# Fifty one-column matmuls ahead of TensorE's first transposition, and a new fixed order of all engines

## The chip, the cores and the metric

The kernel runs on one core of one Trainium2 chip. A core has five engines that run side by side: TensorE (PE, with its weight loads shown apart as PEld), VectorE (DVE), ScalarE (ACT), GpSimd (POOL) and SyncE (SP). SP, and in places POOL and ACT, issue DMA transfers. The metric is the device time of one execution in microseconds (us), lower is better. Times are medians of several executions; the profile is of one more execution.

## The reference, cut to what matters

Two stages follow each other. The first is a retention layer without softmax over 8 batches, 8 heads, 576 positions and 64 values a head; its output, 4608 tokens of 512 values, goes through a two-layer network whose gate is h times cos(h).

```python
scores = scale * np.matmul(q, k.transpose(0, 1, 3, 2))          # scale = 1/8
ret = scores * Dmat                 # gamma_h ** (i - j) where i >= j, else 0
x = np.matmul(ret, v).transpose(0, 2, 1, 3).reshape(4608, 512)
h = x @ w_in                        # 512 x 2048
out = (h * np.cos(h)) @ w_out       # 2048 x 512
```

## The kernel before, in words

**Tiling.** The tokens are cut into nine blocks of 512. Block j takes its rows from two batches: a "unit" is one batch and one third of its positions, (batch, part), and two units of one part make a block. For a unit, `load` (L585) brings q, k and v to staging tiles stgq, stgk, stgv (issued by SP). POOL, and for the first units DVE and ACT, scale and cast them to natk, qnat, natv (L624 and L575, at the very start L574 on ACT). natk and qnat are transposed to kt and qt, by TensorE for the first two blocks (`tpe`, L648, against the identity idn) and by DMA for later ones (`txb`). One phase of TensorE, `scores`, multiplies qt and kt; DVE multiplies by the decay mask into pt (L743); the state sums (natv times natk) run in the same phases; another phase, `outputs`, makes the unit's x (pt times natv, qt times the state copies sba, sbb, sbr), which ACT and DVE copy to xt. All these small matmuls are recorded at L694. They have 64 rows and 64 columns of weights and 64 or 128 columns of data, and go through four parts of the array at once. Here such a phase is called an **attention phase**.

**The network.** The first layer reads win (four slabs, loaded by POOL at L888) and xt; blocks 0 to 2 compute it directly (`mlp1`, L908), blocks 3 to 8 with a seven-product scheme (`seven1`, L1037). The second layer reads gt and wout (loaded by POOL at L892) with the same scheme (`wino2`, L1177). Their matmuls have 128 rows, 128 columns of weights and mostly 256 columns of data. Every matmul is two instructions on TensorE's instruction stream, the weight load and the multiplication.

**What sets the order.** The program is recorded as tasks of a graph (class `Graph`). A string, `ORDER`, gives every task a rank, two characters each (`lay`). `run` then goes through the tasks with a model of the engines and DMA queues: at each step the engine whose next task by rank can start earliest gets it. Only the resulting order of each engine, the choice of buffers and some added waits go into the program; on the chip, semaphores decide when things start. `run` also holds a model of TensorE's instruction supply: `seen` counts instructions, a block k of 256 is asked for when instruction 128 + 256k starts, and the instructions from 450 + 256k on can start when that block is `usable`. `FETCH` and `SHARES` are numbers of that model.

**Filling.** While TensorE waits early in the program, `emit` calls `warm(n)` (L515), which puts in n matmuls of the constant tile `one` with 512 columns (L517); `fill` (L193) picks n from the length of the gap that the model sees. They write the spare bank `wb`, and their results are not used. The first gap is the one ahead of the first transposition.

Of the kernel before, what the change touches and what calls it, by code (L numbers as in the profile page):

```python
# [99 lines left out]
def ap(t, size, p0, n, off, *dims):  # L100
    return bass.AP(t, p0 * size + off, [[size, n]] + [list(d) for d in dims])
# [29 lines left out]
class Graph:  # L131


    BACKLOG, FIRST = 4000, 6000
    SHARES = (0.65, 0.30)
    FETCH = (3200, 1500, 2550, 2000)
    SINCE = 3000

    def __init__(self, pools):
# [113 lines left out]
    def run(self):  # L253
        self.reset()
        free = {e: 0.0 for e in ("pe", "act", "dve", "pool", "sp")}
        todo = {e: sorted((t for t in self.tasks if t.eng == e), key=lambda t: -t.prio) for e in free}
        seen, usable, whole = 4, {}, [False] * 8
        dma_free, port_free = 2500.0, {"dve": 0.0, "pool": 0.0}
        est, order, last, mode, held = {t: 0.0 for t in self.tasks}, [], None, "", None
        slow = sum(t.eng == "pool" and t.dma is not None for t in self.tasks)  # L260
# [111 lines left out]
class Kernel:  # L372
# [10 lines left out]
    SLABS = ((0, 'q', 0, 100), (2, 'q', 1, 101), (1, 'k', 1, 102), (3, 'k', 1, 103))  # L383
    NEXT = 2
    ORDER = (
        "#####$#$#$#%#%#$#######%#&#&#%#$#&#'#)#(#'#)#,#+#'#.#7#/#*#/#'#+#*#,#(#-#.#&#&#%#*#)#(#-#(#)#*#0#2#0#1#3"
        "#2#1#,#7#V#8#/#7#'#(#,#)#-#.#G#@#K#H#*#0#/#L#C#J#G#+#2#1#+#N#O#K#L#M#N#P#E#S#P#T#H#Q#,#3#5#f#[#^#R#-#8#6"
        "#b#W#V#L#.#<#;#5#+#4#U#I#S#3#-#5#E#>#E#6#.#6#@#8#>#4#5#<#=#4#?#<#3#;#>#6#=#H#A#J#;#2#:#:#1#9#B#9#@#9#0#8"
        "#C#=#C#R#G#R#F#?#F#Q#F#P#I#B#I#D#<#D#A#:#A#?#;#B#M#D#O#4#7#9#:#/#>#=#0#?#@#1#A#G#6#m#o#j#k#m#l#l#_#r#u#s"
        "#a#`#_#d#y#p#^#i$'#w#]#Q#[#v#b#s$'#l$%$/#s$/#Z#N#W$3#v$1#e#Z#c$+#r$-#j#^#h$$#i#{#x#d#u$.#q$0#_#S#]$1#t$."  # L390
        "#[#O#X$(#m$&#W#J#T#{#h#|#\\#T#\\$*#n$)#Y#M#Y$&#k$(#|#g#x$,#p$+#X#K#U#y#f#z#a#U#`#z#j$##c#X#f#w#c#t#i#]#g$)"
        "#o$*#Z#b#V#a#q#e#o#n#`#d#Y#q#t#r#k#p#e#g#h#\\$#$%$$#n#u#v#8$-$0#w#O#2#D#B#5#I#C#3#E#H#<$5$7$7$9$8$3$6#z$?"
        "$$$#$@$%#|#4#9#F#K#7#J#N#=#;#M#L#C#:#>#O#R#A#Q#T#?#@#S#P#F$>$B$?$<$A$@$F$,$+$G$'$&$\\$?$Z$O$0$I$[$>$V$_$C"
        "$[$S$6$Q$U$7$P$K$*$D$Z$=$U$J$($G$M$-$J$L$1$L$R$5$N$Q$3$K$Y$<$T$X$:$R$T$@$Y$2$4$,$6$5$;$>$=$4$8#x$2$:$:$;"
        "$<#y$9$=#{$A$D$B$C$E$C#`$H$I$)#P$N$H$F$.$/$P$2$4$V$;$9$W$8$S#B#G#W#Z#E#X#V#D#M#Y#`#Q#J#N#^#a#H#c#[#I#L#\\"
        "#d#V$]$X$W$B$A$b$D$G$c$E$^$o$l$k$M$R${$Y$Z$|$W$s#S#K#f#l#R#e#j#U#X#g#o#[#T#\\#i#t#Y#w#x#W#Z#k#q#g%'$w$x$^"
        "$a%.$l$m%/$f$|#U$E#]$M#_$d#b$n$`$b$e$f$`$F$k$J$f$K$i$n$N$r$p$b#p$p$m$Q#h$y$V$t$s$O$t$P$x$U$r$v$S$z$u$[#n"
        "$w$q$X#m%($_$y%%$\\%&$]%*$e%#%)$`%-${$j#s%+$z$d#r%1$k%(%,$c%3$i%2$h%%%0$g%4%&$n#v%6%'$p#u%9$q%.$]$_$\\$a$c"
        "$o$O$g$d$e$H$^$a$h$h$i$I$g$j$L$l$m$j%#%$$v#o$q$u$T#f%)%+%1%/%=$r%>$s%@$v%5%A$t%D%8%%$(%B%4%,$*%L%$%?%E$y"
        "%G$|%M%#%>%H${%K%<%($&%N%=%.$)%P%&%A%S%*%U%-%Y%1%G%V%2%]%H%7$,%Z%F%<$.%d%=%P%[%3%_%6%`%9%L%^%5%c%K%>$1%e"  # L400
        "%N%E$2%g%?%Q%$%*%0%2%:%6%9%7%5%7$o%:%?%3%<%F$z%;%C$w%O%T%B%I%J%;$&%X%\\%4#q%8%-%,$u$x%Q%)%'%R%+%@#d#]#{#y"
        "#a$$#z#^#e$##|#i#b#k$%$0#h$3$-#_#c$'$+#v%W%D%C%/%0%a%8%:%b%;%J%M%S%V%T%k%B%m%D%o%G%[%n%C%q%Y%H$8%r%Z%K$<"
        "%u%M%b%z%N%{%O&'%S%e&$%P&(%d%W$?&%%c%Z$A&-%Y%i&&%R&)%U&*%T%f&,%V&3%j%`$C&.%h%c$D&6%e%q&/%X&1%]&2%\\%k&4%^"
        "&9%p%h$F&7%n%d$E&>%i%v%E%I%U%X%^%]%W%\\%f%i%A%p%x%`%l%t%L%j%s%I&#&+%g%y%|%a$?&0&5%_$=%h%O%R%@%F%v%Q%[%w%J"
        "%_#l#m$7$/#n$:$5#p#j$4$6#|#s#t$9$=#w$@$B#r#u$;$>$+&8%o%m%b%a&<%f%l&=%g%r%s%u%{%x&@%j&E%o&C%n%|&D%m&I&%%x"
        "$H&H&$%v$G&O%u&,&M%s&P%w&V&#&/&Q%y&W&1&($N&U&.&&$K&a&+&;&X&$&Y&%&[&'&6&]&*&c&5&1$P&\\&4&2$R&h&5&A&b&,&g&0"
        "&i&3&=&f&/&j&?&8$S&k&<&9$U&t&:&D%l%t%w&#&)%y&+&'&;&?%k&A&B%z&G&L%q&:&F%p&R&Z&0&K&N&*$7&^&`&-$:&J&&&(%r%t"
        "&S%z%{&T%|&-$-$6#z$4$I$L$%$,$8$0$J$O$##y#x#{$W$[$9&_&2&3&)&d&e&.&7&8&9&>&:&l&4&n&7&q&<&F&o&6&r&C&K$\\&s&B"
        "&@$Y&y&?&G&u&;&v&=&z&D&Q&x&A'&&K&L$_&{&H&C$X'*&I&R'#&B')&E'(&G&V''&F'/&W&O$`',&P&M$^'6&P&\\'4&N'5&Q'8&T&f"
        "'7&R';&]&X$a':&^&[$b'>&Z&h&@&E&I&L&M&J&S&N&m&p&>&|'$&O'%'-&J&w'+&H'0'2&Y'.'3&X$@'9'=&V$>$1$$$2$'$Q$V$)$5"  # L410
        "$*$($M$T$3$.$<$/$]$Z$;'1&[&T&Z&U'<&S&_&U&`&b&c&e&d'?&W'A&Y'B&\\&i'E&^'K&n&j$e'D&k&g$d'O&c&q'F&]'H&_'P&d&t"
        "'I&`'N&p&e$c'L&r&k$f'U&i&x'M&b'T&h'Q&o'#'W&l'[&w&p$g'Y''&y$i'^&r&{'Z&n'a&t'`&s'$']&q'b&|&u$h'f'+&z$j'e&v"
        "'&&a&l&j&m&g&v&s&o'@'G&a'S'V&u'R'X&m'C'J&f'\\'c'%'_'d'($A'i'j'#$C&y&z')','*'/'-'0'g'h&w&x'o'p'.$E$B'k'n&{"
        "&|'l'm'$'q'r'1'2$F$D's't'3'%'&'v'u'5'4$H$G"
    )
# [59 lines left out]
    def emit(self, order):  # L475
# [217 lines left out]
    def mm(self, out, lhs, rhs, start=True):  # L693
        return lambda e: e.matmul(out(), lhs(), rhs(), start=start, stop=True, skip_group_check=True)  # L694
# [191 lines left out]
    def load_w(self, which, s, gate, prio):  # L886
# [4 lines left out]
        else:  # L891
# [459 lines left out]
```

## Time and profile before

| | |
|---|---|
| median of 3 executions | 282.84 us (282.12 to 283.46) |
| the profiled execution, its own time | 284.13 us |
| its span, first to last instruction | 282.4 us |
| TensorE busy | 270.7 us (96%), 4136 matmuls |
| VectorE, ScalarE, GpSimd busy | 80%, 63%, 57% |
| read from HBM, written | 36.70 MB, 9.44 MB |

The profiled execution took 1.29 us more than the median, and 1.73 us of it lie outside the span. In the timeline each row is a start (us from the span's start), a length, an engine, a line of the kernel, the tiles out<-in, the shape and how many instructions; in brackets stand the idle time of the engine ahead of the row and what ended it. "issue" there means that nothing in the profile held the engine back. A row's length runs to the end of its last matmul, and rows of TensorE overlap by some 0.17 us, since matmuls are pipelined.

### The profile page before, as it was taken

The numbers are of one execution on the slowest core, as the hardware profiler recorded it, in microseconds if no ns is written. First come the engines' busy times: TensorE is split into PE (matmuls) and PEld (weight loads), VectorE is DVE, ScalarE is ACT, GpSimd is POOL, SyncE is SP. The second block draws the span as 40 slices with busy tenths as digits, with TensorE's granted clock in tenths as the row PEclk, the third lists the DMA queues.
The fourth block names the chain that finished last, engine by engine and source line by source line (L and its number), as shares of the span: only waits on it lengthen the run. The fifth ranks groups of instructions, "written<-read, shape, count | busy, mean of one in ns | idle before, by whom it ended". The sixth has DMA issues, their size and how long they took to land.

```text
span 282.4 us, 9745 instructions
## 1 busy us (share of the span) xinstructions
PE 270.7 (96%) x4136; PEld 219.9 (78%) x4136; DVE 227.3 (80%) x394; ACT 177.5 (63%) x367; POOL 161.2 (57%) x180
## 2 busy tenths in 40 slices
PE   6779989999999999979999999999999999999995
PEld 2457568888885468868888888888888888888884
DVE  3666889988974998868997996688759899997764
ACT  4346767255247765669469875885778865778530
POOL 4640872167377683897568757981375667216330
DMA  7999999999999999999999997979816090410016
GB/s 199 249 192 262 273 171 163 300 243 263 179 187 245 204 264 206 181 221 176 251 192 208 279 238 134 168 194 175 194 32 123 6 163 2 159 69 0 2 74 224
DMA packets 122731, 49.91 MB, mean 177 GB/s; under 512 B 84800, under 2 KB 118592, under 8 KB 122688
## 3 DMA queue, kind: packets, MB, share of 16 engines
q1 hardware_dynamic: 118176, 44.84, 74.8%
q0 software_dynamic: 4224, 4.19, 9.6%
q8 instruction: 32, 0.52, 0.8%
q10 hardware_dynamic: 288, 0.26, 0.3%
q14 instruction: 11, 0.09, 0.1%
HBM read 36.70 MB, written 9.44 MB: 163 GB/s over the span
## 4 chain that ended last, share of the span: by engine, by line
PE 84%; DMA 8%; POOL 3%; issue 2%; SPq 1%; DVE 1%; ACT 1%; DVEq 0%; ACTq 0%
PE bk L1177 38%; PE bk L1037 26%; PE bk L908 11%; PE bk L694 8%; DMA stgq<-in_q_dram 3%; DMA win<-in_moe_w_in_dram 3%; DMA stgk<-in_k_dram 3%; POOL natv L624 1%; SPq L585 1%; POOL qnat L624 1%; POOL gt L1026 1%; POOL win L888 0%; ACT xt L574 0%; DVE sq L1020 0%; PE bk L648 0%
## 5 line engine op out<-in xcount | busy, mean ns | idle before, releaser
L1026 POOL TENSOR_TENSOR gt<-sq,cb 128x512 bf16<-128x512 f32 x48 | 55.8, 1172 | 49.1 <-ACT cb L1022 27.0
L908 PE MATMUL bk<-xt,win 128*128 128x256 bf16 (+1 forms) x288 | 46.3, 308 | 1.8 <-DMA win<-in_moe_w_in_dram 0.9
L624 POOL TENSOR_TENSOR natv<-stgv,wv 128x512 bf16<-128x512 f32 x36 | 37.5, 1046 | 12.5 <-DVE s L1108 4.8
L920 DVE TENSOR_TENSOR gt<-bk,cb 128x256 bf16<-128x256 f32 (+1 forms) x72 | 34.5, 507 | 12.0 <-ACT cb L917 9.3
L917 ACT ACTIVATE cb<-bk 128x256 bf16<-128x256 f32 (+1 forms) x72 | 31.2, 455 | 19.6 <-PE bk L908 16.5
L624 POOL TENSOR_TENSOR qnat<-stgq,wq 128x512 bf16<-128x512 f32 x32 | 33.5, 1052 | 16.7 <-DVE s L1114 5.6
L1037 PE MATMUL bk<-xt,win 128*128 128x256 bf16 x288 | 41.0, 273 | 0.0
L1020 DVE TENSOR_TENSOR sq<-bk,sq 128x512 f32<-128x512 f32 x48 | 32.5, 684 | 8.9 <-PE bk L1037 5.0
L908 PEld LDWEIGHTS bk<-xt,win 128*128 128x128 bf16 x288 | 26.8, 98 | 15.3 <-DVE pt L743 1.2
L743 DVE TENSOR_TENSOR pt<-bk,tr 128x512 bf16<-128x512 f32 x48 | 31.1, 682 | 8.4 <-PE bk L694 8.1
L575 POOL CAST natk<-stgk 128x512 bf16<-128x512 f32 x34 | 20.7, 614 | 28.2 <-DMA stgk<-in_k_dram 15.7
L1177 PE MATMUL bk<-wout,gt 128*128 128x256 bf16 x288 | 36.7, 273 | 0.0
L1026 DVE TENSOR_TENSOR gt<-bk,cb 128x512 bf16<-128x512 f32 x48 | 32.3, 682 | 4.0 <-ACT cb L1022 3.8
L1177 PE MATMUL bk<-wout,s 128*128 128x256 bf16 x288 | 35.6, 273 | 0.0
L1177 PE MATMUL bk<-tw,s 128*128 128x256 bf16 x288 | 35.4, 273 | 0.0
L574 ACT ACTIVATE sq<-bk 128x512 f32<-128x512 f32 x48 | 27.7, 595 | 10.0 <-PE bk L1037 8.8
L1022 ACT ACTIVATE cb<-sq 128x512 bf16<-128x512 f32 x48 | 30.0, 632 | 5.4 <-DVE sq L1020 2.9
L1022 ACT ACTIVATE cb<-bk 128x512 bf16<-128x512 f32 x48 | 28.4, 598 | 6.7 <-PE bk L1037 3.7
L1177 PEld LDWEIGHTS bk<-tw,s 128*128 128x128 bf16 x288 | 28.0, 98 | 3.6 <-DVE pt L743 0.3
L1037 PEld LDWEIGHTS bk<-xt,win 128*128 128x128 bf16 x288 | 27.9, 98 | 3.6
L1177 PEld LDWEIGHTS bk<-wout,gt 128*128 128x128 bf16 x288 | 27.6, 98 | 3.7 <-issue 0.2
L1177 PEld LDWEIGHTS bk<-wout,s 128*128 128x128 bf16 x288 | 27.7, 98 | 3.5
(80 smaller groups left out, 436.5 us busy)
## 6 DMA issues: line engine op xcount, KB each, us to landing
stgq<-in_q_dram SPq DMA_DIRECT2D x16, 512.0 KB, 6.1
out_dram<-os SPq DMA_DIRECT2D x16, 512.0 KB, 4.4
stgk<-in_k_dram SPq DMA_DIRECT2D x20, 256.0 KB, 5.6
stgv<-in_v_dram SPq DMA_DIRECT2D x20, 256.0 KB, 5.4
stgk<-in_k_dram SPq DMA_DIRECT2D x6, 512.0 KB, 6.9
stgv<-in_v_dram SPq DMA_DIRECT2D x6, 512.0 KB, 7.4
win<-in_moe_w_in_dram POOLq DMA_DIRECT2D x4, 512.0 KB, 8.0
wout<-in_moe_w_out_dram POOLq DMA_DIRECT2D x4, 512.0 KB, 7.5
```

What stands on the lines that cost most here:

```text
L574: return self.one(eng, dur, lambda e: e.activation(dst(), src(), AF.Copy), r=r, w=w, **kw)
L624: self.one(eng, 610 if eng == "dve" else 1030, lambda e, out=out, inp=inp, tab=tab, col=col, hs=hs: e.tensor_tensor(out(), inp(), ap(tab, ...
L694: return lambda e: e.matmul(out(), lhs(), rhs(), start=start, stop=True, skip_group_check=True)
L743: self.one("dve", 610, lambda e, r=r, b=b, pt=pt: e.tensor_tensor(ap(self.at(pt), 1024, 0, 128, 512 * r, [64 * ny * ny, 8 // ny // ny], [1 ...
L908: inst = e.matmul(ap(self.at(bk), 512, 0, 128, 0, [1, n]), ap(self.WIN, 4 * DFF, 0, 128, c * DFF + 128 * f, [1, 128]), ap(self.at(xt), 204 ...
L917: self.one("act", n - 15, lambda e: e.activation(ap(self.at(cb), TB, 0, 128, 0, [1, n]), ap(self.at(bk), 512, 0, 128, 0, [1, n]), AF.Sin, ...
L920: self.one("dve", 75 + n / 0.96, lambda e: e.tensor_tensor(ap(self.at(gt), NF * TB, 0, 128, f * TB + 256 * h0, [1, n]), ap(self.at(bk), 51 ...
L1020: self.one("dve", 610, lambda e: e.tensor_tensor(half(src), self.at(bank).ap(), half(src), ALU.add), r=[(bank,)], w=four(src))
L1022: self.one("act", 530 if name else 490, lambda e: e.activation(self.at(cb).ap(), ap(self.at(src), size, 0, 128, 0, [1, 512]), AF.Sin, bias ...
L1026: self.one(eng, 1120 if name else 610, lambda e: e.tensor_tensor(ap(self.at(gt), NF * TB, 0, 128, (8 * n + 2 * g) * TB + 256 * h, [TB, 2], ...
L1037: inst = e.matmul(ap(self.at(bank), 512, 0, 128, 256 * f, [1, 256]), l(c, f), rr(c), stop=True, skip_group_check=True, start=(first and f ...
L1177: inst = e.matmul(place(bank, tt), l(f, tt), rr(f), stop=True, skip_group_check=True, start=(first and f == 0 and tt < len(bank)))
```

## The change

The class's numbers change, `emit` calls a new function `pad` ahead of TensorE's first task (and still `warm`), `fill` picks fewer large matmuls for the first gap, the planner's count starts 100 instructions later, and `ORDER` is another string of the same length, so that nearly every engine's order differs.

```diff
-    BACKLOG, FIRST = 4000, 6000
-    SHARES = (0.65, 0.30)
-    FETCH = (3200, 1500, 2550, 2000)
+    BACKLOG, PAD = 4000, 50
+    SHARES = (0.80, 0.35)
+    FETCH = (3200, 1500, 3550, 5550)
...
-        return int(0.6 * (gap - 150) / 220 if seen else (gap - 1400) / 430)
+        return int(0.6 * (gap - 150) / 220 if seen else (gap - 3000) / 430)
...
-        seen, usable, whole = 4, {}, [False] * 8
+        seen, usable, whole = 4 + 2 * self.PAD, {}, [False] * 8
...
-                    usable[k] = max(a + self.FETCH[0], dma_free + self.FETCH[1]) + self.FETCH[2] + self.FETCH[3] * (a < 45000)
+                    usable[k] = max(a + self.FETCH[0], dma_free + self.FETCH[1] * (a > 8000)) + self.FETCH[2 + (8000 < a < 45000)]
...
     ORDER = (
-        "#####$#$#$#%#%#$#######%#&#&#%#$#&#'#)#(#'#)#,#+#'#.#7#/#*#/#'#+#*#,#(#-#.#&#&#%#*#)#(#-#(#)#*#0#2#0#1#3"
+        "###$###$#$###%#$#####%#%#&#&#%#$#%#'#(#'#(#)#*#)#'#,#*#-#+#/#'#+#,#.#)#/#.#&#&#&#+#(#*#-#(#)#*#0#1#1#2#0"
...
             if t.eng == "pe":
                 gap = t.start - warm
+                if not warm:
+                    self.pad(self.G.PAD)
                 if gap > 400 and self.wb.left:
...
+    def pad(self, n):
+        def mm(e):
+            for _ in range(n):
+                inst = e.matmul(ap(self.at(self.wb), 512, 0, 1, 0, [1, 1]), ap(self.ONE, 128, 0, 128, 0, [1, 1]),
+                                ap(self.ONE, 128, 0, 128, 0, [1, 1]), start=True, stop=True, skip_group_check=True)
+            return inst
+        self.P.add("pe", mm, r=["one"], w=[("bk", self.wb.slot)])
```

Lines of the changed kernel are ten higher than before from `emit` on (L648 is L658, L694 is L704, L908 is L918, L1037 is L1047, L1177 is L1187). The numbers of real matmuls stay the same; of the matmuls on `one` there were 24 of 512 columns and are 20, and the 50 of one column come on top, so the program has 46 matmuls, or 92 instructions, more ahead of all that follows.

**Place 1, the start of TensorE.** Before, the thirteen fillings are followed by the transposition of k:

```order
L517 MATMUL bk<-one 128x512 x13
L648 MATMUL bk<-idn,natk 128x128 x4
L648 MATMUL bk<-idn,qnat 128x128 x8
L648 MATMUL bk<-idn,natk 128x128 x4
L517 MATMUL bk<-one 128x512 x2
L694 MATMUL bk<-qt,kt 64x128 x16
```

In the changed kernel, the pads and five fillings stand there, then both halves of q:

```order
L519 MATMUL bk<-one 1x1 x50
L527 MATMUL bk<-one 128x512 x5
L658 MATMUL bk<-idn,qnat 128x128 x8
L527 MATMUL bk<-one 128x512 x2
L658 MATMUL bk<-idn,natk 128x128 x8
L527 MATMUL bk<-one 128x512
L704 MATMUL bk<-qt,kt 64x128 x32
```

Eight fillings gave way to fifty pads, and the transpositions of q moved ahead of those of k. On POOL, which issues the loads of win, the first casts stood like this before:

```order
L575 CAST natk<-stgk 128x512
L624 TENSOR_TENSOR natv<-stgv,wv 128x512
L575 CAST natk<-stgk 128x512
L624 TENSOR_TENSOR natv<-stgv,wv 128x512
L888 DMA win<-in_moe_w_in_dram 128x4x512 x2
```

Now, on POOL at the same place:

```order
L585 CAST natk<-stgk 128x512
L634 TENSOR_TENSOR natv<-stgv,wv 128x512 x2
L585 CAST natk<-stgk 128x512
L898 DMA win<-in_moe_w_in_dram 128x4x512 x2
L634 TENSOR_TENSOR natv<-stgv,wv 128x512 x2
```

The second cast of k changed places with the second scaling of v; the same four operations stand ahead of the first load of win. SP's first twelve loads keep their order.

**Place 2, the first attention work of unit (2, 0).** TensorE before, from the last transpositions for block 1 to that unit's state sums and scores, with work of both layers between:

```order
L648 MATMUL bk<-idn,qnat 128x128 x4
L908 MATMUL bk<-xt,win 128x256 x4
L1177 MATMUL bk<-wout,gt 128x256 x8
L908 MATMUL bk<-xt,win 128x256 x4
L648 MATMUL bk<-idn,natk 128x128 x4
L1177 MATMUL bk<-tw,s 128x256 x16
L908 MATMUL bk<-xt,win 128x256 x8
L1177 MATMUL bk<-tw,s 128x256 x8
L694 MATMUL bk<-natv,natk 64x64 x16
L694 MATMUL bk<-qt,kt 64x128 x16
L1177 MATMUL bk<-wout,s 128x256 x8
```

TensorE in the changed kernel, up to the same state sums and scores:

```order
L918 MATMUL bk<-xt,win 128x256 x12
L658 MATMUL bk<-idn,natk 128x128 x4
L918 MATMUL bk<-xt,win 128x256 x8
L658 MATMUL bk<-idn,qnat 128x128 x4
L918 MATMUL bk<-xt,win 128x256 x8
L658 MATMUL bk<-idn,qnat 128x128 x4
L918 MATMUL bk<-xt,win 128x256 x8
L704 MATMUL bk<-natv,natk 64x64 x16
L918 MATMUL bk<-xt,win 128x256 x4
L704 MATMUL bk<-qt,kt 64x128 x16
L1187 MATMUL bk<-wout,gt 128x256 x8
```

The attention work came 56 matmuls of the real work earlier, ahead of all of the second layer, and is cut in two by four matmuls of the first.

**Place 3, the middle of the program.** TensorE before, from the products of one unit to the scores and state sums of the next:

```order
L694 MATMUL bk<-pt,natv 64x64 x32
L694 MATMUL bk<-qt,sba 64x64 x12
L694 MATMUL bk<-natv,natk 64x64 x16
L694 MATMUL bk<-qt,sba 64x64 x12
L1177 MATMUL bk<-wout,s 128x256 x16
L1037 MATMUL bk<-xt,win 128x256 x4
L1037 MATMUL bk<-xs,tx 128x256 x4
L694 MATMUL bk<-qt,kt 64x64 x32
L694 MATMUL bk<-natv,natk 64x64 x16
L1037 MATMUL bk<-xt,tx 128x256 x4
```

TensorE in the changed kernel, the same work:

```order
L704 MATMUL bk<-pt,natv 64x64 x32
L704 MATMUL bk<-qt,sba 64x64 x12
L704 MATMUL bk<-natv,natk 64x64 x16
L704 MATMUL bk<-qt,sba 64x64 x12
L1187 MATMUL bk<-wout,s 128x256 x16
L1047 MATMUL bk<-xt,win 128x256 x4
L704 MATMUL bk<-qt,kt 64x64 x32
L704 MATMUL bk<-natv,natk 64x64 x16
L1047 MATMUL bk<-xs,tx 128x256 x4
L1047 MATMUL bk<-xt,tx 128x256 x4
```

Here four matmuls of the network moved behind the scores; counted from the program's start, the row of scores begins at matmul 1812 before and 1854 now (the first is number 0).

Over the whole program, TensorE goes from the network to an attention phase and back 30 times from unit (2, 0) on, and 33 times in the changed kernel.

More of the change, by code (lines that the diff above doesn't have):

```diff
@@ L391 @@
[L391 to L410, printed above, removed]
@@ new lines @@
+        "#3#3#,#6#3#7#0#5#'#(#,#)#-#.#G#A#I#G#*#/#0#K#C#M#I#+#2#1#+#O#Q#L#K#N#M#P#E#S#f#T#I#Q#,#5#3#V#K#Z#O#-#9#6"
+        "#]#R#`#V#.#8#:#2#-#6#U#J#S#E#?#D#<#5#@#5#/#4#;#4#:#4#.#8#D#=#C#A#;#?#=#6#<#9#7#;#?#9#=#>#8#>#:#2#9#8#1#7"
+        "#B#<#B#J#F#O#F#@#E#N#G#P#H#B#H#@#:#A#L#D#J#C#>#F#R#H#R#4#7#;#<#0#>#=#3#@#A#/#D#B#8#e#m#`#c#j#h#c#W#r#x#s"
+        "#_#`#X#e#o#n#^#l#u#z#k#]#i#y#e#x#w#c#v#|#k$$#g#[#f$'#m$'#b#Z#g$/#r$-#d#X#_$,#u$0#v#b#t$0#t$2#W#L#T#z#h#{"
+        "#^#S#[$-#s$.#[#P#W$+#q$,#\\#Q#Y$&#l$%#p#^#m#{#g#|#u#a#s$(#o$*#Y#N#U$##i$##X#M#V$$#j$&#a#U#]$)#n$(#_#T#\\$*"
@@ L415 @@
+        "'J&_'N&r&f$d'L&n&j$e'T&m&y'P&e'S&i'Z&r'$'Y&l'`&z&s$g'W&w&v$i'f&w'+'X&k'^&p'_&q'''\\&o'a&{&u$h'b'*&z$j'd&t"
+        "'(&g&j&h&l&t&p&i&s'?'A&`'D'U&v'O'[&n'Q'R&g'c'e'%'V']&x$@'h'i'#$B&|'&','-'#')'/'0'g'j&y&x'k'o'.$C$F'm'n&|"
+        "&{'l'p'$'q'r'2'1$E$D's't'3'%'&'v'u'5'4$H$G"
     )
@@ L895, in load_w @@
         self.one("pool", 1000, fn, r=gate, w=[(which, s)] if which == "win" else [(which, s, 0), (which, s, 1)],
-                 sem=f"{which}{s}", dma=2750 if which == "win" else 3000, tail=900, prio=prio)
+                 sem=f"{which}{s}", dma=3350 if which == "win" else 3450, tail=500, prio=prio)
     def mlp1(self, j, f, ses, prio):
```

28 lines of the change are left out of this document (20 added, 8 removed).

## The prediction

> **What bounds the kernel now.** I read the page first, for which engine is full, then the chain that ended last, then TensorE's timeline for the places where it stands still.
>
> ```profile
> PE 270.7 (96%) x4136; PEld 219.9 (78%) x4136; DVE 227.3 (80%) x394; ACT 177.5 (63%) x367; POOL 161.2 (57%) x180
> DMA  7999999999999999999999997979816090410016
> q8 instruction: 32, 0.52, 0.8%
> ```
>
> The third row (packets, MB, share of 16 engines) is not what I expected to need. 4136 matmuls and 4136 weight loads on 32 packets are 258 instructions a packet, of 16 KB each: TensorE's program comes to it by DMA in pieces, over engines that the DMA row shows full (a digit is a fortieth of the span, 7 us) for some 200 us.
>
> The chain's early part, in order of time (start, length, what):
>
> ```profile
> 10.45 0.61 POOL natk L575
> 11.06 1.00 POOL natv L624
> 12.06 0.89 POOL win L888
> 12.95 8.27 DMA win<-in_moe_w_in_dram
> 21.70 8.43 DMA stgq<-in_q_dram
> 32.23 2.05 POOL natv L624 x2
> ...
> 38.69 0.76 ACT xt L574
> ```
>
> Up to 34.3 us the end is set by transfers: POOL issues the loads of win, the landing of the second at 21.2 lets SP load unit (0, 1), and POOL's scaling of that ends at 34.3. From there to the end the chain lies on TensorE. Now TensorE's timeline, the rows ahead of and behind each pause:
>
> ```profile
> 1.12 4.82 PE L517 MATMUL bk<-one 128*128 128x512 bf16 x13 [1.12 <-DVE lg L543]
> 7.48 0.40 PE L648 MATMUL bk<-idn,natk 128*128 128x128 bf16 x4 [1.54 <-ACT natk L574]
> 17.71 1.47 PE L908 MATMUL bk<-xt,win 128*128 128x256 bf16 x12 [0.88 <-DMA win<-in_moe_w_in_dram]
> 20.40 0.50 PE L908 MATMUL bk<-xt,win 128*128 128x256 bf16 x3 [0.68 <-issue]
> 37.22 0.28 PE L694 MATMUL bk<-natv,natk 64*64 64x64 bf16 x7
> 38.22 0.22 PE L694 MATMUL bk<-natv,natk 64*64 64x64 bf16 x3 [0.71 <-issue]
> 123.73 0.26 PE L694 MATMUL bk<-natv,natk 64*64 64x64 bf16 x9
> 125.45 0.25 PE L694 MATMUL bk<-natv,natk 64*64 64x64 bf16 x7 [1.46 <-issue]
> ```
>
> The last three pauses (0.68, 0.71 and 1.46 us) fall inside a run of equal matmuls and end by "issue": no data was missing. Here is how many matmuls (behind the x) had started by each:
>
> ```profile
> 0.00:20.30 20.30, 14.67 (x221) 1.00 1.01 214
> 20.30:38.10 17.80, 16.82 (x246) 1.00 1.09 243
> 38.10:125.30 87.20, 85.59 (x1386) 1.00 1.13 221
> ```
>
> Two instructions to a matmul make 492 and 2772 between the pauses. With the separate waits that the program holds (100 on TensorE), 512 and 2816 fit, 2 and 11 times 256. I take the pauses for **borders of instruction blocks**: TensorE had used up one block and the next had not come. There are 31 such borders, one in 123 to 126 matmuls, and three of them cost 2.85 us together. When do they cost something? The same view over some stretches of about one block (stretch, length, busy time and count of PE, the granted clock, the share of the DMA engines, GB/s):
>
> ```profile
> 32.62:37.50 4.88, 4.74 (x111) 1.00 0.86 199
> 50.00:55.00 5.00, 5.00 (x127) 1.00 1.18 308
> 119.85:123.99 4.14, 4.14 (x138) 1.00 1.14 263
> 156.75:161.37 4.62, 4.62 (x128) 1.00 1.20 290
> 125.30:265.00 139.70, 139.09 (x2152) 1.00 0.70 142
> ```
>
> ```profile
> 239.80 1.34 PE bk L694 x128
> ```
>
> Ahead of the second pause 111 matmuls went in 4.9 us, ahead of the third 138 in 4.1, where as many large ones at 0.108 us (worked out below) would take 15. Two other blocks as quick, to 55 and to 161 us, paused nowhere. The last row of the second fence, from the chain, is 128 small matmuls in 1.34 us without a pause, at a time when the DMA row is near 1. So a border can hurt where a block is used up in 4 to 5 us and DMA is full, and one in three such blocks did so in the middle of the program.
>
> A rule speaks against this reading. The Trainium skill, "Runtime: NRT & Kernel Launch", section "Instruction fetch mechanics", agrees on blocks of 256 instructions of 16 KB, but says that the fetch of the next is hidden because instructions are issued more slowly than they are supplied. The 1.46 us row disagrees, as I read it; by the page the pauses would have another cause and stay, which is a rival below.
>
> **The change, part by part.** The sum is made against the profiled execution's own 284.13 us; the median of the runs shown is 282.84, or 1.29 lower.
>
> *The pads and the shorter filling: 0 (0 to +2.2).* The pads stand in TensorE's first gap. No row has a one-column matmul. Downwards, 16 small ones take 0.24 us from 113.83 to 114.07 (quoted below), 15 ns each, or 0.75 us for fifty. Upwards, each could cost the longest full weight load on this tile:
>
> ```profile
> L517 PEld LDWEIGHTS bk<-one x24: 96/98/152, 1.1 to 19.0; 128*128 128x128 bf16 x24
> 5.07 1.29 DVE L624 TENSOR_TENSOR qnat<-stgq,wq 128x512 bf16<-128x512 f32 x2 [1.22 <-DMA stgq<-in_q_dram]
> ```
>
> At 0.152 us that is 7.6 us; with the start at 1.12 and five fillings of 0.37 (1.9 us) they would end at 10.6, 3.1 later than the first transposition at 7.48, of which the 0.88 us wait at 17.71 takes up a part: +2.2. A one-column matmul has less to load and to stream than the small row, so I take near that, 1 to 2.5 us. Then pads and fillings end by 5.5, before q's halves are ready (5.7 and 6.4 by the row above), whose transpositions now go ahead of k's, which wait until 7.48 as before. That wait hides the pads. There is no gain, since transfers set this stretch.
>
> *The first casts on POOL: -0.3 (0 to -0.6).* POOL stands still for 0.67 us ahead of the second cast of k, and the second scaling of v now fits in there:
>
> ```profile
> 8.73 1.04 POOL L624 TENSOR_TENSOR natv<-stgv,wv 128x512 bf16<-128x512 f32 x1 [1.29 <-ACT qt L574]
> 10.45 0.61 POOL L575 CAST natk<-stgk 128x512 bf16<-128x512 f32 x1 [0.67 <-DMA stgk<-in_k_dram]
> ```
>
> So the loads of win, and with them the chain to 34.3, can start up to 0.6 us sooner; DMA is full, so I take half.
>
> *The first pause: 0 (0 to -0.68).* 46 more matmuls ahead put this border at matmul 221 of the new order, in scores of unit (1, 0), ahead of the first product with win, where TensorE waits for DMA anyway (0.88). What it frees is then late on the transfers that end at 34.3.
>
> *The second pause: -0.7 (0 to -0.71).* Its border stays in the same phase (467 is one matmul into the row that starts at 466). But the block ahead of it now holds 49 small matmuls, 16 transpositions and some 56 of the network, 32 of them with 512 columns, twice 0.108: some 11 us of work, where 4.9 us stood before. What is late next is xt, whose copy follows this phase in the chain (38.69), so the gain passes on.
>
> *Border 3: +0.4 (0 to +1.46).* Some 123 matmuls on, at about 590, the next border falls into natv,natk of unit (2, 0) (place 2). Its block holds 67 small matmuls, 16 transpositions and 40 large ones, some 6 us of work, while wout is loaded. This is the second pause's case a block later; by that row it would cost 0.7, and I take a little over half.
>
> *The third pause: -1.46 (0 to -1.46).* The border near 1853 now falls on the last network matmul ahead of the scores (place 3). The block ahead of it has 72 small matmuls and 56 large ones, 7 us instead of 4.
>
> *New quick blocks: +0.6 (0 to +4.4).* By the order, three blocks of the changed kernel are used up in under 5 us while DMA is full: those that end near matmuls 1344, 1979 and 2482 (about 80, 130 and 160 us). The last holds 100 small matmuls and 24 large, 4 us, like the one that paused 1.46. Before, one in three paused, so I expect one pause of 1.46 at a chance of a half, 0.7, rounded down.
>
> *More changes between network and attention phases: +0.6.* From unit (2, 0) on there are 33 instead of 30. One costs 0.2 us, which these rows give:
>
> ```profile
> 113.03 0.60 PE L1037 MATMUL bk<-xs,tx 128*128 128x256 bf16 x4
> 113.56 0.45 PE L694 MATMUL bk<-qt,kt 64*64 64x64 bf16 x32
> 113.83 0.30 PE L694 MATMUL bk<-natv,natk 64*64 64x64 bf16 x16
> 114.07 0.61 PE L1037 MATMUL bk<-xs,win 128*128 128x256 bf16 x4
> 118.01 0.60 PE L1037 MATMUL bk<-xs,win 128*128 128x256 bf16 x4
> 118.44 0.60 PE L1037 MATMUL bk<-xt,win 128*128 128x256 bf16 x4
> ```
>
> Four large matmuls last 0.43 to the next large ones (118.01 to 118.44), 0.108 each, and 0.53 to small ones; 32 small ones last 0.27, so 16 should last 0.13, and last 0.24 to the next large ones. Nothing hides this, as TensorE is full.
>
> *The rest of the new order: 0 (0 to +1).* From 125.3 to 265 us TensorE was busy for 139.09 of 139.70 us (windows above): it hardly waits for another engine, and DVE at 80% has room. That the new order is as close I can only bound: each wait costs its length.
>
> Sum: -0.3 - 0.7 + 0.4 - 1.46 + 0.6 + 0.6 = -0.86, so 283.27 by the profile's own time, and 282.0 by the median.
>
> **The rivals.** *No new border pauses.* The terms +0.4 and +0.6 go: 281.0. For it: 28 of 31 borders pass now without a pause, two of them after quick blocks. Against: the three new quick blocks and border 3. *The new borders pay in full* (the slower side). The fetch of a block waits behind data, and border 3 and the three quick blocks each cost the 1.46 of the third pause: +5.84 instead of +1.0, so 286.8. It decides from 3.3 us of new pauses on, a little over two of the four. *The change does not do what it says*: the pauses are not block borders and only their place moves. They then stay, and -0.3 and +0.6 remain: 283.1. This is where the skill's rule would lead. *The clock.* The first thirteen fillings take 0.37 us each on the mean, later ones less:
>
> ```profile
> 9.63 0.82 PE L517 MATMUL bk<-one 128*128 128x512 bf16 x3
> ```
>
> That is 0.27 each. So the array begins at a lower pace. If pads do not count as work and the first sixteen products with win run at half pace, 0.216 instead of 0.108 us, it costs 1.7: 283.7. The Trainium skill, "TensorE: Matmul & The Clock Gate", Part 1, has the array at half clock until about 3.4 us of steady work, and so leans to this rival; the trace shows slow fillings to 5.9 us (1.12 and 4.82), and no run here shows what pads do.
>
> **How the numbers follow.** Forecast 0.42, no new pause 0.30, new borders in full 0.14, pauses that are not borders 0.09, clock 0.05. Half a per cent, 1.4 us, is about what a measurement of this kernel can tell from no change. Faster by more means under 281.43: most of the second case and the lower edge of the first, 0.33. Slower by more means above 284.25: the third case and a little of the others, 0.17. The rest, 0.50, lies within. The range reaches from the second case less the rest of the casts and of the changes of phase (281.0 - 0.8 = 280.2) to the forecast with border 3 in full and one more full pause (282.0 + 1.06 + 1.46 = 284.5).
>
> **What would show it.** The first transposition row would start at or before 6.4 us and the first product with win at or before 17.7. No "issue" row would stand near 20 and in the phase at 36 to 38, a small one in natv,natk at 42 to 44, none in the scores at 123 to 126, and at most one of the three quick blocks would pause. "Issue" pauses in total would fall from 2.85 to 1 us. Waits of TensorE for DVE, ACT or POOL of over 1 us in all behind 45 us would make the prediction wrong, and so would pauses at counts of matmuls that do not fit 256 instructions.

## The result, and the profile after

The changed kernel took 284.95 us (median; 283.86 to 289.72), the kernel before, on the same chip, 283.32 (282.12 to 284.96). The ratio is 1.0061, with a 95% interval of 1.0031 to 1.0090: slower by 0.9 to 2.5 us, where 282.0 was forecast. Timed again on another chip the changed kernel took 283.83 and the one before 283.43, ratio 1.0024 (1.0000 to 1.0049). The ratios leave out slow executions, which lie over 1.5% above the fastest of their kernel (289.72 here, two of some 290 in one experiment below). So the loss is small, some 0.2 to 0.6%, on the second chip hardly clear of nothing, and on the other side of zero than the forecast. The profiled execution took 285.73 us by itself, with a span of 284.0, where before it was 284.13 and 282.4.

The page, engines and instruction queue: TensorE is as full as before, and one more block of instructions is fetched.

```profile
PE 273.8 (96%) x4182; PEld 220.4 (78%) x4182; DVE 225.5 (79%) x394; ACT 176.7 (62%) x367; POOL 162.9 (57%) x180
q8 instruction: 33, 0.54, 0.8%
```

TensorE's timeline of the changed kernel, rows of the start and those with a wait that matter below, in the columns of the rows shown before:

```profile
1.12 1.39 PE L519 MATMUL bk<-one 128*1 128x1 bf16 x50 [1.12 <-DVE lg L553]
2.44 2.31 PE L527 MATMUL bk<-one 128*128 128x512 bf16 x5
5.85 1.21 PE L658 MATMUL bk<-idn,qnat 128*128 128x128 bf16 x8 [1.10 <-DVE qnat L634]
7.71 1.06 PE L658 MATMUL bk<-idn,natk 128*128 128x128 bf16 x8
8.56 0.63 PE L527 MATMUL bk<-one 128*128 128x512 bf16 x1
17.50 0.60 PE L918 MATMUL bk<-xt,win 128*128 128x256 bf16 x4 [0.34 <-DMA win<-in_moe_w_in_dram]
35.77 0.42 PE L704 MATMUL bk<-qt,kt 64*64 64x128 bf16 x16 [0.20 <-DVE pt L753]
37.58 0.64 PE L704 MATMUL bk<-pt,natv 64*64 64x128 bf16 x32 [0.27 <-DVE pt L753]
39.65 1.47 PE L918 MATMUL bk<-xt,win 128*128 128x256 bf16 x12 [0.17 <-ACT xt L584]
101.96 0.32 PE L704 MATMUL bk<-natv,natk 64*64 64x64 bf16 x16 [0.25 <-POOL natv L634]
115.53 0.61 PE L1047 MATMUL bk<-xs,win 128*128 128x256 bf16 x4 [0.30 <-POOL win L954]
127.18 0.61 PE L1047 MATMUL bk<-xs,win 128*128 128x256 bf16 x4 [0.55 <-ACT sq L584]
148.39 0.45 PE L704 MATMUL bk<-pt,natv 64*64 64x64 bf16 x32 [0.52 <-DVE os L1176]
161.59 0.25 PE L704 MATMUL bk<-natv,natk 64*64 64x64 bf16 x6 [0.22 <-issue]
```

The pauses that end by "issue" at 20, 38 and 125 us are gone; a new one of 0.22 stands at 161. In their place stand rows that end by DVE, POOL or ACT: TensorE waits for data. Before, from 45 us to the end, TensorE had one more row with an idle time of 0.2 us or more beside the third pause:

```profile
152.20 0.45 PE L694 MATMUL bk<-qt,kt 64*64 64x64 bf16 x32 [0.20 <-issue]
```

With the 1.46 us of the third pause that makes 1.66 us. The changed kernel's last five rows above sum to 1.84: what the border gave there, the waits took.

Since executions of one kernel differ by some us, each kernel was profiled three times (the later four are among the experiments). The spans were 282.4, 281.7 and 281.9 before, and 284.0, 282.3 and 281.7 changed. The next table is worked out from TensorE's rows: the time at which it had done the same amount of real work (matmuls at full pace, without those on `one`), as a mean of the three.

| real work done, us | 22 | 50 | 80 | 100 | 247 |
|---|---|---|---|---|---|
| before, at us | 40.6 | 69.7 | 102.7 | 125.2 | 278.0 |
| changed, at us | 40.5 | 70.3 | 104.1 | 125.4 | 278.6 |
| changed later by | -0.1 | +0.6 | +1.4 | +0.2 | +0.6 |

The changed kernel loses from 41 to 103 us, gets 1.2 back at the pause at 125 us that it no longer has, and loses some again later. These are the places that the experiments look at. Between the columns 22 and 80 TensorE goes to an attention phase and back 15 times, and 11 times before: at the 0.2 us of the prediction's rows, 0.8 of the 1.4 lost there. The rest is near what TensorE stood still there in the three profiles, 0.35, 1.09 and 0.51 us, at 90 or at 102 us.

### The profile page after: what moved, and what is told of

It reads as the page before. It is cut to its first block, busy times and chain, and to the rows that moved or that the text cites. A ratio compares the mean times of both kernels' runs of the same rounds, so it can differ in the third digit from the quotient of the medians.

```text
span 284.0 us, 9853 instructions
## 1 busy us (share of the span) xinstructions
PE 273.8 (96%) x4182; PEld 220.4 (78%) x4182; DVE 225.5 (79%) x394; ACT 176.7 (62%) x367; POOL 162.9 (57%) x180
## 4 chain that ended last, share of the span: by engine, by line
PE 67%; DMA 8%; SPq 6%; DVE 6%; POOL 6%; issue 5%; ACT 1%; POOLq 0%; ACTq 0%
PE bk L1187 30%; PE bk L1047 24%; DMA stgv<-in_v_dram 8%; PE bk L918 7%; PE bk L704 6%; SPq L673 3%; SPq L595 3%; POOL natv L634 3%; DVE pt L753 2%; DVE s L1124 1%; DVE s L1118 1%; POOL natk L585 1%; POOL tx L954 1%; PE bk L658 1%; POOL qnat L634 1%
## 5 line engine op out<-in xcount | busy, mean ns | idle before, releaser
L634 POOL TENSOR_TENSOR natv<-stgv,wv 128x512 bf16<-128x512 f32 x36 | 38.1, 1066 | 16.6 <-DMA stgv<-in_v_dram 6.9
L918 PE MATMUL bk<-xt,win 128*128 128x256 bf16 (+1 forms) x288 | 46.7, 308 | 0.8 <-DMA win<-in_moe_w_in_dram 0.3
L1047 PE MATMUL bk<-xt,win 128*128 128x256 bf16 x288 | 40.8, 273 | 0.0
L927 ACT ACTIVATE cb<-bk 128x256 bf16<-128x256 f32 (+1 forms) x72 | 30.6, 456 | 13.9 <-PE bk L918 10.5
L918 PEld LDWEIGHTS bk<-xt,win 128*128 128x128 bf16 x288 | 26.4, 98 | 14.3 <-issue 1.5
L1187 PE MATMUL bk<-wout,s 128*128 128x256 bf16 x288 | 36.4, 273 | 0.0
L1187 PE MATMUL bk<-wout,gt 128*128 128x256 bf16 x288 | 36.2, 273 | 0.0
L1187 PE MATMUL bk<-tw,s 128*128 128x256 bf16 x288 | 35.7, 273 | 0.0
L584 ACT ACTIVATE sn<-bk 128x512 f32<-128x512 f32 (+1 forms) x29 | 16.3, 568 | 28.0 <-PE bk L1187 27.2
L1176 DVE TENSOR_TENSOR os<-bk,sn 128x512 f32<-128x512 f32 (+1 forms) x28 | 18.6, 668 | 15.7 <-PE bk L1187 10.9
L1187 PEld LDWEIGHTS bk<-wout,gt 128*128 128x128 bf16 x288 | 27.9, 98 | 3.5
L1187 PEld LDWEIGHTS bk<-tw,s 128*128 128x128 bf16 x288 | 27.7, 98 | 3.7
```

Source lines behind the costliest of these rows:

```text
L584: return self.one(eng, dur, lambda e: e.activation(dst(), src(), AF.Copy), r=r, w=w, **kw)
L634: self.one(eng, 610 if eng == "dve" else 1030, lambda e, out=out, inp=inp, tab=tab, col=col, hs=hs: e.tensor_tensor(out(), inp(), ap(tab, ...
L918: inst = e.matmul(ap(self.at(bk), 512, 0, 128, 0, [1, n]), ap(self.WIN, 4 * DFF, 0, 128, c * DFF + 128 * f, [1, 128]), ap(self.at(xt), 204 ...
L927: self.one("act", n - 15, lambda e: e.activation(ap(self.at(cb), TB, 0, 128, 0, [1, n]), ap(self.at(bk), 512, 0, 128, 0, [1, n]), AF.Sin, ...
L1047: inst = e.matmul(ap(self.at(bank), 512, 0, 128, 256 * f, [1, 256]), l(c, f), rr(c), stop=True, skip_group_check=True, start=(first and f ...
L1187: inst = e.matmul(place(bank, tt), l(f, tt), rr(f), stop=True, skip_group_check=True, start=(first and f == 0 and tt < len(bank)))
```

## The experiments

**Are the pauses borders of instruction blocks, and what do the pads do?** Two kernels part the change: the new order without its pads, and the old order with them.

```diff
# the changed kernel: no pads
-                if not warm:
-                    self.pad(self.G.PAD)
```

> The changed kernel with the fifty pads left out on the chip; the order, the fillings and the planner's numbers stay. Theory (borders and waits): the new order loses time by waits of TensorE for other engines, and the pads only place its block borders. Without them every border falls 50 matmuls later in the order's work, into quick blocks (about 18, 86 to 91, 125 and 163 us), so pauses that end by issue grow from 0.2 to 1.5 to 3 us and the time from 285.0 to 286 to 288. Rival 1 (the pads cost the time, by delaying the first transpositions or keeping the array at its lower pace): 283.3, as before. Rival 2 (borders do not matter): 285.0, with the same waits.

```diff
# the kernel before: fifty pads
+                if not warm:
+                    self.pad(50)
```

> The kernel before with fifty pads ahead of TensorE's first work and nothing else changed. Theory (borders): the pauses at 20, 38 and 125 us (2.85 us) go, and new ones of about 1 us each come where the shifted borders end quick blocks (about 16 and 24 us, 84 and 107, 153 and 158, 190 us), so the time is 283 to 286. Rival 1 (the pads cost the time): 285.0 with pauses at the old matmuls. Rival 2 (pauses are not block borders): the pauses stay at the same work, 283.3.

The new order without pads: 284.26 us, ratio to before 1.0058 (1.0029 to 1.0086), as with them; the 286 to 288 that was expected did not come. The old order with pads: 1.0015 (0.9993 to 1.0037), no difference. So the loss goes with the new order, and the pads neither cost nor gain time as a whole, to within the 0.3% or so of these intervals. But they move the pauses. TensorE's timeline of the new order without pads has them in other places than with pads:

```profile
38.34 0.22 PE L702 MATMUL bk<-natv,natk 64*64 64x64 bf16 x2 [0.64 <-issue]
101.87 0.22 PE L702 MATMUL bk<-qt,sba 64*64 64x64 bf16 x3 [0.48 <-issue]
```

and in the old order with pads the three at 20, 38 and 125 are gone, for one of 1.72 that was not there before:

```profile
151.54 0.29 PE L704 MATMUL bk<-natv,natk 64*64 64x64 bf16 x13 [1.72 <-issue]
```

Nothing but fifty matmuls on a constant was added, so the rival that the pauses have another cause falls. The trace's packets on the instruction queue say more. Each of these pauses stands at instruction 450 + 256k of TensorE (with k a whole number, counted in the trace), and ends soon after a packet of that queue has landed:

| kernel | instruction | packet landed | TensorE goes on | later by | pause |
|---|---|---|---|---|---|
| before | 962 | 36.82 | 38.22 | 1.40 | 0.71 |
| before | 3778 | 123.84 | 125.45 | 1.61 | 1.46 |
| old order, 50 pads | 4802 | 149.99 | 151.54 | 1.55 | 1.72 |
| new order, no pads | 962 | 36.99 | 38.34 | 1.35 | 0.64 |
| new order, no pads | 3010 | 100.51 | 101.87 | 1.36 | 0.48 |
| changed | 5058 | 160.14 | 161.59 | 1.45 | 0.22 |

Borders without a pause mostly came later than that behind their packet (4.6 us, for instance, at instruction 1218 before), though the soonest in each of these four profiles came 1.45 to 1.99 us behind it. The Trainium skill, "Runtime: NRT & Kernel Launch", section "Instruction fetch mechanics", has the fetch hidden behind execution; here it is mostly, but not in the rows of the table.

Two more counts of pads tried how well the borders' cost can be foretold.

```diff
# the changed kernel
-                    self.pad(self.G.PAD)
+                    self.pad(14)
```

> The changed kernel with 14 pads in place of 50, nothing else. From the packets of the instruction queue in the six traces so far, TensorE can go on some 1.4 us after a block's packet has landed. By that model this count puts borders into the quick blocks that end near 91 and 162 us, so two pauses of 1 to 2 us each stand there and the time is 287 (286 to 288). Rival (where the borders fall does not matter for the whole, since waits for other engines take over what a pause leaves): 285.

```diff
# the kernel before
+                if not warm:
+                    self.pad(14)
```

> The kernel before with 14 pads and nothing else. By the model of the packets the pauses at 38 and 125 us shrink to 0.2 to 0.4 us each, and others of up to 0.5 come near 18 and 152 us: 282.5 (282.0 to 283.2). Rival (pads cost time of their own): 283.3 or more.

New order: 1.0079 (1.0045 to 1.0113), or 285.5 us, where 287 was expected and 285 was the rival's. By the two ratios of the changed kernel that is 0.5 or 1.6 us above the order with fifty pads: not settled. Its profiled execution, of 290.0 us, has a pause of 1.77 us at 94 us, where one was expected near 91, and only 0.12 at 166 us for the other. Old order: 283.02 us, ratio 0.9978 (0.9953 to 1.0004): at the forecast's side, not clear of nothing. Its pauses, expected at 0.2 to 0.4 us, did not shrink as far:

```profile
38.78 0.21 PE L704 MATMUL bk<-qt,sbb 64*64 64x128 bf16 x1 [0.57 <-issue]
```

```profile
124.97 0.24 PE L704 MATMUL bk<-qt,kt 64*64 64x64 bf16 x5 [0.70 <-issue]
```

This is the quickest version found, and no proven gain.

**Is the loss in the first part or the later one?** Two hybrids take one order for all tasks that the planner starts before 50 us, and the other for the rest (another table in `ORDER`; the pads set so that the borders of the later part stay where they were).

> The changed kernel's order for all tasks that its planner starts before 50 us, the order of before for the rest, no pads (so that the borders of the rest fall within one matmul of where they fell before). Theory (the loss lies behind 50 us): 283.3 to 284.3, with the pause of about 1.5 us at 125 us back and no wait for another engine over 0.3 us behind 50 us. Rival (the loss lies in the start): 285 or more.

> The order of before for all tasks that its planner starts before 50 us, the changed order for the rest, 46 pads (so that the borders of the rest fall as in the changed kernel). Theory (the loss lies behind 50 us): 284.5 to 286, with the waits for ACT, DVE and POOL at about 115, 127 and 148 us there again, 1.3 us in all, and no pause at 125 us. Rival (the loss lies in the start): 283 or less.

They took 1.0116 (1.0093 to 1.0138) and 1.0109 (1.0082 to 1.0135) of before, both slower than either whole order. New waits for DVE stand behind the seam of both: in the first, 0.8 us for pt at 81, in the second 1.2 us in two for gt, the longer at 63. Both forecasts missed (283.3 to 284.3 and 284.5 to 286), and so they tell nothing of the two orders' shares: half of one order and half of the other do not make one.

**How far do pauses and waits repeat?** Both kernels once more, unchanged.

> The kernel before once more, for a second profile. Theory (the borders of the old order cost it): pauses that end by issue again near 20, 38 and 125 us, 2 to 3 us in all; waits of TensorE for other engines behind 45 us again under 0.3 us each. Rival (the first profile was a chance): the pauses differ by over 1 us in all.

> The changed kernel once more, for a second profile. Theory (the new order holds the waits): the waits near 102, 115, 127 and 148 us stand there again, over 1.2 us in all. Rival (they come and go with the landing of transfers): at most the one at 115 is there, as in the run without pads, and the span is 282.5 to 283.

> The kernel before a third time, for a third profile. Theory: pauses by issue near 20, 38 and 125 us, 2 to 3 us in all, and no wait for another engine over 0.3 us behind 45 us. Rival: no pause at 125 us, so that the first two were chance.

> The changed kernel a third time, timed on the same chip as the kernel with v first, and for a third profile. Theory: 284.5 to 285.3, a wait for natv at 102 us and one for win at 115 us there again, those at 127 and 148 us not, pauses by issue behind 17 us under 1 us in all. Rival: the waits at 127 and 148 us (1.1 us) are the rule.

The second profile of before, TensorE's timeline, and then the third:

```profile
37.70 0.22 PE L694 MATMUL bk<-natv,natk 64*64 64x64 bf16 x3 [0.24 <-issue]
124.87 0.25 PE L694 MATMUL bk<-natv,natk 64*64 64x64 bf16 x7 [1.52 <-issue]
```

```profile
21.20 0.50 PE L908 MATMUL bk<-xt,win 128*128 128x256 bf16 x3 [1.51 <-issue]
125.13 0.25 PE L694 MATMUL bk<-natv,natk 64*64 64x64 bf16 x7 [0.91 <-issue]
```

The pause at 125 us repeats (0.9 to 1.5); those at 20 and 38 come and go. In all the three executions show 2.85, 1.76 and 2.42 us of pauses, 2.3 on the mean. The changed kernel, second and third profile:

```profile
35.35 0.42 PE L704 MATMUL bk<-qt,kt 64*64 64x128 bf16 x16 [0.20 <-DVE pt L753]
37.16 0.64 PE L704 MATMUL bk<-pt,natv 64*64 64x128 bf16 x32 [0.26 <-DVE pt L753]
102.24 0.32 PE L704 MATMUL bk<-natv,natk 64*64 64x64 bf16 x16 [1.09 <-POOL natv L634]
115.80 0.61 PE L1047 MATMUL bk<-xs,win 128*128 128x256 bf16 x4 [0.30 <-POOL win L954]
```

```profile
90.05 0.23 PE L704 MATMUL bk<-qt,sba 64*64 64x64 bf16 x5 [0.51 <-issue]
114.95 0.61 PE L1047 MATMUL bk<-xs,win 128*128 128x256 bf16 x4 [0.23 <-POOL win L954]
159.33 0.25 PE L704 MATMUL bk<-natv,natk 64*64 64x64 bf16 x6 [0.30 <-issue]
```

Its pauses sum to 0.32, 0 and 0.81 us, 0.4 on the mean (the first with 0.10 at 90 us). The waits for pt at 35 and 37 us (the third profile has 0.20 and 0.27) and for win at 115 are there each time. Those for ACT and DVE at 127 and 148 us (1.1 us) are in the first profile alone, so they belong to that execution. Without it the spans are 282.3 and 281.7, no longer than the three of before. The third timing, expected at 284.5 to 285.3 us, came to 283.83, and the wait at 102 us that was expected there is missing. And the wait at 102 us and the pause at 90 take each other's place: where TensorE lost 0.51 at the border, natv was there when it came; where it lost nothing, it waited 1.09. The chain of waits from 60 to 135 us bears on why. Before, second profile, the chain is TensorE's throughout but for two copies of ACT; some of its pieces:

```profile
94.45 0.95 PE bk L694 x80
95.42 0.74 ACT xt L574
...
123.35 1.52 issue
```

Changed, second profile:

```profile
70.48 0.38 PE bk L704 x16
70.89 1.29 DVE pt L753 x2
...
77.21 1.05 POOL qnat L634
78.78 1.05 POOL natv L634
80.12 2.17 SPq L673
82.33 3.90 DMA stgv<-in_v_dram
87.91 2.09 POOL tx L954
91.60 1.93 SPq L673
93.58 4.92 DMA stgq<-in_q_dram
98.57 2.06 POOL qnat L634 x2
101.19 1.01 POOL natv L634
102.24 0.45 PE bk L704 x32
```

From 71 to 102 us TensorE does not set the end: DVE, POOL's casts, SP's transposes behind these and the loads behind the transposes do. What TensorE gains in that stretch, it waits off at 102 us. Not in every execution: with the pause at 90 us, in the third profile, the chain stayed on TensorE up to 108 us, and in the third profile of before a part of it, too, lay on SP and DMA, though TensorE waited there for 0.3 us at most.

**What makes natv late?** First, POOL's four sums of win (one is in the chain at 87.91) went to DVE, with their places in `ORDER`.

```diff
-    TXENG = ("pool", "dve", "pool", "dve")
+    TXENG = ("dve", "dve", "dve", "dve")
```

> The changed kernel with the four sums of win that POOL makes (2.12 us each) on DVE instead (0.7 us each), at the same places of the program. Theory (in the new order the chain between 71 and 116 us runs over POOL and SP, and TensorE waits for it): POOL's casts, the transposes behind them and the loads behind those come up to 2 us earlier, the waits at 102 (0.25 and 1.1 us in two profiles) and at 115 us (0.3) go, and the time falls by 0.7 to 1.5 us against the changed kernel: 283.5 to 284.3. Rival (the time is lost by the changes of phase and in the start): 285.

> The same edit in the kernel before, whose chain from 60 to 135 us lies on TensorE alone. Theory: no gain, 283.3 (282.8 to 283.8), as POOL sets nothing there. Rival (POOL's load slows both orders alike): 282.0 to 282.6.

New order: 1.0078 (1.0058 to 1.0098), no gain on the changed kernel's 1.0061 or 1.0024. The wait at 115 us went, as expected, but that at 102 stayed:

```profile
102.44 0.32 PE L704 MATMUL bk<-natv,natk 64*64 64x64 bf16 x16 [0.76 <-POOL natv L634]
```

So that half of the theory falls: POOL's sum is in the chain, but without it the transposes take as long to get through. The old order lost by the same edit, 1.0041 (1.0019 to 1.0063). Then TensorE alone was changed: its phase at 102 us was put off.

```diff
# rows of TensorE, the changed kernel
-MATMUL bk<-xt,win 128x512 x16
+MATMUL bk<-xt,win 128x512 x24
 MATMUL bk<-pt,natv 64x64 x32
...
-MATMUL bk<-xt,win 128x512 x8
 MATMUL bk<-xt,win 128x256 x4
```

> The changed kernel with the attention phase at 101 to 102 us (products and state sums of unit (3, 1)) put behind the next eight network matmuls of 512 columns, 1.7 us of work; only TensorE's order changes. Theory: the wait for natv at 102 us goes (0.25 to 1.1 us), but the chain over DVE and POOL to 115 us goes on from there, so the wait for win at 115 us stays or grows to 0.5 to 1, and the time is 284.5 to 285. Rival (that wait alone was the loss): 284.0.

1.0084 (1.0063 to 1.0105). The wait only moved 2 us on, to the copies that follow the phase:

```profile
104.20 0.61 PE L1047 MATMUL bk<-xt,win 128*128 128x256 bf16 x4 [0.84 <-DVE xt L585]
```

Last, the load itself was moved. Before the change, v of that unit, (3, 1), was issued at 91.48 us, there too behind q and k, and TensorE used natv at 104.7; in the changed kernel it was issued at 94.58, behind q and k, and used at 101.96.

```diff
# rows of SP, the changed kernel
+DMA stgv<-in_v_dram 128x8x64
 DMA stgq<-in_q_dram 128x8x128
-DMA stgk<-in_k_dram 128x8x64
-DMA stgv<-in_v_dram 128x8x64
-DMA stgk<-in_k_dram 128x8x64 x2
+DMA stgk<-in_k_dram 128x8x64 x3
# rows of POOL
+TENSOR_TENSOR natv<-stgv,wv 128x512
 TENSOR_TENSOR qnat<-stgq,wq 128x512 x2
 CAST natk<-stgk 128x512
-TENSOR_TENSOR natv<-stgv,wv 128x512
```

> The changed kernel with one load moved: on SP, v of unit (3, 1) goes ahead of q and k of that unit, and on POOL its scaling to natv ahead of the casts of q and k. TensorE, DVE and ACT keep their order. Theory (the load order of the new order makes natv of that unit late, and TensorE waits for it): v lands near 98.5 instead of 100.8, natv is ready near 100, and the wait at 102 us (0.25 to 1.1 us) goes; since nothing else on TensorE is late, the time falls by 0.5 to 1 us to 284.0 to 284.5, unless the wait turns up again at 115 us. Rival (DMA alone limits: whatever is loaded first, something else is late): the wait goes to another place by 116 us and the time stays at 285.

The wait at 102 us is gone; from 85 to 140 us TensorE's timeline has one wait left:

```profile
114.99 0.61 PE L1047 MATMUL bk<-xs,win 128*128 128x256 bf16 x4 [0.29 <-POOL win L954]
```

So with v in front the wait goes. But the time did not follow: 1.0023 (1.0000 to 1.0046), beside 1.0024 for the changed kernel on the same chip, with medians of 284.44 and 283.83 us. The expected 0.5 to 1 us is not there, so this wait is no large part of the loss in most executions.

**What do the extra phase changes cost?** Four of the new order's cut phases were joined (one of them shown).

```diff
# rows of TensorE, the changed kernel, near 78 us
-MATMUL bk<-qt,kt 64x128 x16
-MATMUL bk<-wout,s 128x256 x8
-MATMUL bk<-qt,kt 64x128 x16
+MATMUL bk<-wout,s 128x256 x8
+MATMUL bk<-qt,kt 64x128 x32
```

> The changed kernel with four of its attention phases that network work cuts in two joined again (the network work between the parts goes ahead of the first part; near 44, 68, 78 and 87 us). Theory (a change of phase costs 0.2 us, and behind it the supply sets the time until 116 us): TensorE is busy for 0.8 us less, but the wait at 102 us grows by as much, 285.0 (284.6 to 285.2). Rival (TensorE's own work sets the time): 284.2.

1.0167 (1.0141 to 1.0194), or 3 to 4 us slower than the changed kernel by its two ratios: a clear miss. Worked out from TensorE's rows, what the phase changes cost fell from 8.85 to 7.99 us in all, as expected. But new waits stand where the cuts had been, for the banks and masks that ACT and DVE had cleared meanwhile, two of them:

```profile
72.01 0.42 PE L704 MATMUL bk<-qt,kt 64*64 64x128 bf16 x16 [0.75 <-ACT sn L584]
80.95 0.42 PE L704 MATMUL bk<-qt,kt 64*64 64x128 bf16 x16 [0.80 <-DVE pt L753]
```

A cut in a phase costs 0.2 us, and here the network work in it covered more than that.

## Why the prediction was wrong

The sum put the forecast at -0.86 us; by the three profiled executions of each it is +0.7 on the mean, and by the medians +0.4 and +1.6. Its mechanism, block borders, was right, and so was their total: the pauses fell by 2.0 us on the mean, where a fall from 2.85 to 1 was forecast. What failed is the term that it set at nothing, the rest of the new order, which came to 1.9 us, and with it the step that what the second pause frees is gained.

- **Pads, 0: right.** Fifty took 1.32 us (1.12 to 2.44), 26 ns each, in the estimate of 1 to 2.5, and the wait for q hid them: the first transposition began at 5.85 us behind a wait of 1.10, and without pads at 5.88 behind one of 2.45. Without them the time was the same.
- **Casts on POOL, -0.3: nothing came of it.** The first load of win was issued at 11.28 instead of 12.00 and TensorE's first product with it started 0.2 us sooner, but at 41 us both kernels stand at the same work.
- **The first pause, 0: right;** it went and gave nothing.
- **The second pause, -0.7: the step failed.** The prediction said that xt, whose copy follows the phase, is late next, "so the gain passes on". The pause went, and the product that waits for xt began at 39.65, before at 39.57. What was late in the new order was the masks ahead of the copy: the two waits for pt, 0.20 and 0.27 us, stand in all three profiles. They stand in the new order without pads too, which has the pause (0.64 us at 38.34), so they belong to the order. On the mean of three profiles the product began 0.1 us sooner than before. And the pause itself was 0.71, 0.24 and nothing in the three profiles of before.
- **Border 3, +0.4: no pause** in any of the three profiles.
- **The third pause, -1.46: right.** The table's row shows it: 1.4 us late at 103 us, 0.2 at 125. The pause itself was 1.3 us on the mean of three profiles.
- **New quick blocks, +0.6: about right.** Two of the three paused, 0.10 and 0.22, then 0.51 and 0.30 us in the third profile, none in the second.
- **Phase changes, +0.6: right**, 0.76 as worked out from the rows (8.08 to 8.84 us in all, mean of three); but they do not fall evenly: four more by 103 us, one less behind.
- **The rest of the new order, 0 (0 to +1): the step that turned the sign.** Pauses fell by 2.0 us on the mean (2.34 to 0.38), phase changes cost 0.76, and the spans rose by 0.67. So the rest is 0.67 + 1.96 - 0.76 = +1.9. The step took the row of 139.09 of 139.70 us busy, which belongs to the old order, as a sign of the new one. In the new order TensorE waits for pt at 35 to 37 us, for natv at 102 (0 to 1.1), for win at 115 (0.2 to 0.3), and in one execution of three for 1.1 more at 127 and 148: 1.5 us on the mean of the three.

Of the rivals, "no new border pauses" came nearest in mechanism (0.4 us of pauses), but its time of 281.0 was the furthest off of all from the first result: it too took every pause that goes as gained. The prediction had named the sign of being wrong, over 1 us of waits for DVE, ACT or POOL behind 45 us; there were 1.6 in the first profile, 1.4 in the second and 0.2 in the third. The clock rival had its slower pace but not its price: behind pads and five fillings eight transpositions still took 0.85 us (7.71 to 8.56), 0.106 each, and without the pads 0.85 too (7.74 to 8.59), where before, behind thirteen fillings, four took 0.24 at the same time. So the pads had not quickened it. But this lay beside the transfers, and by the first products with win, at 17.50, the pace was full (four in 0.53 to the next small row). The Trainium skill, "TensorE: Matmul & The Clock Gate", Part 1, with half clock until about 3.4 us of steady work, fits the pace of these rows; the granted clock of these stretches reads 1.00 in both kernels.

Behind 41 us the account nearly closes: 0.6 for the three phase changes more, 1.1 for the waits (natv 0.45, win 0.28, the first profile's 1.07 shared by three) and 0.4 for pauses, less 1.3 for the third pause, make 0.8, where the table has 0.7 (from -0.1 to +0.6). Ahead of 41 us, pauses of 1.05 us on the mean went and 0.1 was gained.

What stays open: what took the gain ahead of 41 us beyond the 0.47 of the waits for pt, and which part of the order would have to change. Moving v took the wait at 102 us away, yet did not move the median. The waits for pt were not tried by themselves. And the ratio of the two kernels was 1.0061 on one chip and 1.0024 on another, with executions of each some 3 us apart.

## What to carry to other kernels

For each stall that a change takes away, look up what arrives next at the waiting engine, and how much later that is than the stall's end; only what lies between is gained, and here that was nothing at 38 us and nearly all at 125. A row of the old profile that shows an engine without waits says nothing of a new order: give the new order's waits a term of their own, with bounds as wide as the stalls that it removes. And a cut that looks like a cost, such as network work between two halves of a phase, may be the cover of another engine's work: joined, it cost 3 us or more.

## What the runs showed of the hardware

TensorE could go on 1.35 to 1.61 us after its block's packet had landed, in every pause of the table, whichever kernel and place. One-column matmuls follow each other at 26 ns, where the large ones, at 0.108 us for 256 columns, take 0.4 ns a column; the Trainium skill, "TensorE: Matmul & The Clock Gate", section "Wait — 56ns, not 53.3ns?", has some 25 ns as the least distance of two matmuls, and the pads agree. The small ones in four parts of the array go faster, 32 in 0.27 us. And DVE and POOL were both slower side by side in the first profile of the changed kernel, ahead of the wait at 148 us: DVE's sum took 1.53 us and POOL's scaling beside it 1.49. In the second profile the same sum took 0.68 us at 144.21 us, with POOL idle, and the scaling 1.05 at 142.70.

```profile
144.85 1.53 DVE L1124 TENSOR_TENSOR s<-gt 128x1024 bf16<-128x1024 bf16 x1
```

```profile
144.34 1.49 POOL L634 TENSOR_TENSOR qnat<-stgq,wq 128x512 bf16<-128x512 f32 x1
```

That the one slowed the other, and that this made the wait, is argued from these rows and the chain, not tried.
